# Strided sparse attention and a star-ReLU feed-forward: v of the second batch ahead of three quarters of w_out, the first batch's band q and k by head pair, PSUM banks taken as they come free

## The chip, the core and the metric

The kernel runs on one core of a Trainium2 chip. A core has a matrix engine (TensorE, PE in the profile; PEld are its weight loads), a vector engine (VectorE, DVE), a scalar engine (ScalarE, ACT), GpSimd (POOL) and a sync engine (SyncE, SP). Each engine works through its own list of instructions in order, and they wait for each other by semaphores. POOL and SP issue the DMAs here, each on a queue of its own (q0 for POOL, q1 for SP). Matmuls write to PSUM, which has eight banks of 128 partitions x 512 fp32 numbers. The metric is the device time of one execution in microseconds (us).

## The reference

Inputs are q, k, v of 8 batches x 8 heads x 576 positions x 64, weights w_in (512 x 2048) and w_out (2048 x 512), and two numbers s and b. All are fp32.

```python
scores = scale * np.matmul(q, k.transpose(0, 1, 3, 2))
rel = pos[:, None] - pos[None, :]
mask_local = (rel >= 0) & (rel < 32)
mask_strided = (rel >= 0) & (pos[None, :] % 32 == pos[:, None] % 32)
# heads 0 to 3 take mask_local, heads 4 to 7 mask_strided
scores = np.where(mask, scores, -1e9)
attn = exp(scores - max) / (sum + 1e-9)
x = (attn @ v).transpose(0, 2, 1, 3).reshape(4608, 512)
h = x @ w_in
r = np.maximum(h, 0.0)
out = (s * (r * r) + b) @ w_out
```

## The kernel before

**Attention.** A batch has four pairs of heads, m = 0 to 3 (`pair_steps`): two local ("band") pairs and two strided pairs. A band pair is cut into 6 blocks of 96 positions, a strided pair into 8 groups of 72 positions. For each pair PE transposes q and k (`trans`, lines 405 and 413), an engine copies the results from PSUM (q into a block-diagonal tile qD, k into kT), PE computes scores (line 533; in batch 0 after a matmul at line 530 that adds the mask as large negative numbers), ACT takes the exponential (line 551), PE multiplies by v with a column of ones (AV, line 590), DVE takes the reciprocal of the sums (line 605), DVE or ACT scales (lines 616 and 611), PE transposes x (`xtrans`, line 638) and an engine copies it to xT. In later batches some transposes are made by DMA.

**Feed-forward.** The 4608 tokens make 9 blocks of 512. A block's first layer (`ff1`, line 883) is 64 matmuls (16 column groups of w_in times 4 pieces of x); ACT or DVE takes the ReLU (lines 910 and 912) and the square (lines 918 and 920). The second layer (`ff2`, line 941; from block 3 on a scheme with fewer products at line 851) multiplies by w_out. b times the column sums of w_out (`bcs_steps`, lines 968 and 979) is added when the result is taken out of PSUM (line 952), so block 0's results stay in their banks until all of w_out has come. Block 0 needs the x of batch 0 alone; block 1 needs that of batches 0 and 1.

**Order of the work.** A planner (`Plan`) writes the order of all instructions when the program is built. It keeps a clock for PE and estimates of when each engine is free, how long each job takes and when each load lands (`landing`, `arrive`). At each point it emits the first step that is ready by these estimates: attention while it is behind its due time, else first layer, else second layer. Where nothing is ready in the first part of the program, `keep_running` emits filler matmuls (line 1177). A step that opens a group of matmuls needs a PSUM bank. Banks have five tags: t (1 bank), s (2), a (1), f1 (2), f2 (2). `group_of` gives each group one tag, in fixed turns, and within a tag the banks are taken in turn.

**Loads.** POOL issues the loads that convert fp32 to fp16. In the first part its list is: q and k of batch 0's band heads (`load_qk`, line 275, one load of 288 KB each), q, k, v of its strided heads (line 290), a cast of v of heads 0 and 1 (line 317), a small copy at line 1069 that waits for the strided q, w_in in three loads (line 307), a cast of v of heads 2 and 3, and then `second`: w_out chunk 0, q and k of batch 1, w_out chunks 1 to 3 (line 313), v of batch 1 (lines 295 and 290). SP loads v of batch 0's band heads as fp32 (`stage_v`, line 240) into room that w_out fills later: heads 0 and 1 at the start, heads 2 and 3 after a tiny DMA (line 1051) that waits for the band q to land; then the masks, s and b. In tile names this v is called w_out_sb, because it lies there. `ql`, `kl` are band tiles, `qs`, `ks`, `vs` strided ones.

Of the kernel before, what the change touches and what calls it, by code (L numbers as in the profile page):

```python
# [9 lines left out]
FP16 = mybir.dt.float16  # L10
FP32 = mybir.dt.float32
# [4 lines left out]
class Plan:  # L16
# [9 lines left out]
    def __init__(self):  # L26
        self.t = 0.0
        self.done = {}
        self.pend = []
        self.free = {"A": 0.0, "V": 0.0, "P": 7000.0, "D": 0.0, "X": 0.0, "Y": 0.0}  # L30
        self.count = {}

    def ready_at(self, needs):
        if any(k not in self.done for k in needs):
# [6 lines left out]
    def flush(self):  # L41
        while True:
            best = None
            for p in self.pend:
                r = self.ready_at(p[0])
                if r is not None and r <= self.t and (best is None or r < best[0]):
                    best = (r, p)
            if best is None:
                return
            r, p = best  # L50
            self.pend.remove(p)
            eng = min(p[1], key=lambda e: max(self.free[e], r) + p[1][e])
            end = max(self.free[eng], r) + p[1][eng]
            self.free[eng] = end
            p[2](eng)
            for k in p[3]:
                if isinstance(k, Group):
                    k = ("rel", k.tag, k.n)
                soon = isinstance(k, tuple) and k[0] == "soon"
                self.done[k] = end + (6000.0 if soon else p[4] or self.LAT[eng])  # L60

    def step_ready(self, s):
        r = self.ready_at(s.needs)
        if r is None:
            return None
        if s.group is not None:
            n = self.count.get(s.group.tag, 0)
            if n >= s.group.bufs:
                k = ("rel", s.group.tag, n - s.group.bufs)
                if k not in self.done:  # L70
                    return None
                r = max(r, self.done[k])
        return r

    def emit(self, s):
        if s.group is not None:
            s.group.n = self.count.get(s.group.tag, 0)
            self.count[s.group.tag] = s.group.n + 1
        s.fn()
        self.t += s.ns  # L80
        for k in s.keys:
            self.done[k] = self.t + 200.0
        for p in s.posts:
            self.post(*p)
        if s.after is not None:
            s.after()
# [11 lines left out]
class Group:  # L98


    def __init__(self, tag, bufs):
        self.tag, self.bufs, self.n = tag, bufs, None


class Step:
# [6 lines left out]
def kernel(  # L112
# [130 lines left out]
    stage_v(range(2))  # L243
    nc.sync.dma_start(out=negs, in_=h_neg.ap())
    nc.vector.memset(ones16, 1.0)
    nc.vector.memset(part32, 1.0 / 32)
    nc.vector.memset(vl_stage[0:LPAD], 0.0)
    for i in range(2):
        nc.vector.memset(qD_loc[i], 0.0)
        nc.vector.memset(kT_loc[i][:, 0:LPAD], 0.0)  # L250
        nc.vector.memset(qD_str[i], 0.0)
    for i in range(NV):
        nc.vector.memset(v_loc[i][:, :, :, D:D + 1], 1.0)
# [80 lines left out]
    def cast_v(b, loc, mm, key):  # L334
        nt, np_, dst = (LT, 128, v_loc) if loc else (ST, SQ, v_str)

        def g(eng):
            src = vl_stage if loc else loaded[b, "vs"].rearrange(
                "p (h t d) -> p h t d", h=4, d=D)
            for h in range(2 * mm, 2 * mm + 2):  # L340
                copy_on(eng, out=dst[b % NV][0:np_, h, :, 0:D], in_=src[:, h])
        n = nt * D
        plan.post([key], {"P": 1000.0} if loc else {"A": 2 * (170 + 0.83 * n), "V": 540.0}, g,
                  [("cast", b, mm) if loc else ("in", "vs", b, mm)])
        if loc:
            rows_before(b, mm, ("cast", b, mm))

    def rows_before(b, mm, key):
# [5 lines left out]
        def g(eng):  # L354
# [4 lines left out]
    TB, SB, AB, F1B, F2B = 1, 2, 1, 2, 2  # L359
    HEAD_T = 2  # L360
    PE_MASK = 1
    ps = {tag: [psum.tile([128, PS], FP32, name=f"ps_{tag}{i}") for i in range(n)]
          for tag, n in (("t", TB), ("s", SB), ("a", AB), ("f1", F1B), ("f2", F2B))}

    taken = {"a": 0, "t": 0, "s": 0}

    def group_of(kind, b, m, q=False):

        t, a, f1, f2 = ("t", TB), ("a", AB), ("f1", F1B), ("f2", F2B)
        banks = {"a": [a], "t": [t], "s": [("s", SB)]}[kind]  # L370
        if b == 0:
            banks = {"a": [f2, f2, f1], "t": [t, a], "s": [("s", SB), ("s", SB), f1]}[kind]
        elif b == 1 and kind == "a":
            banks = [f1, f1, a]
        elif b >= KB_DMA and kind == "a":
            banks = [a, t]
        elif b == 1 and q:
            banks = [t, f2]
        taken[kind] += 1
        return Group(*banks[taken[kind] % len(banks)])  # L380

    def bank(group):
        return ps[group.tag][group.n % group.bufs]

    def pair_steps(b, m):

# [196 lines left out]
        def av(e, j, group):  # L583
# [13 lines left out]
            if j % per == per - 1:  # L597
# [2 lines left out]
                j0 = j - per + 1  # L600

                def rc(eng):
                    st["rec", e, j] = recp.tile([128, 6, 1], FP32, tag="rec" + group.tag,
                                                bufs=group.bufs, name="rec")
# [386 lines left out]
    def arrive(keys, at):  # L991
        for k in keys:
            plan.done[k] = at
# [81 lines left out]
    for mm, at in (0, 7100.0), (1, 14400.0):  # L1075
# [21 lines left out]

# [64 lines left out]
    def keep_running(until):  # L1162

        ghz = 1.2 if plan.t < 6000 else 2.4
        n = min(int((until - 100.0 - plan.t) * ghz) - 20, 512) // 128
        for tag, bufs in (("f1", F1B), ("s", SB), ("f2", F2B)):
            k = ("rel", tag, plan.count.get(tag, 0) - bufs)
            if k[2] < 0 or plan.done.get(k, until) <= plan.t:
                break
        else:  # L1170
            return False
        if n < 1:
            return False
        out = ps[tag][plan.count.get(tag, 0) % bufs][:, 0:128 * n]

        def f():
            nc.tensor.matmul(
# [90 lines left out]
```

## Time and profile before

| | |
|---|---|
| median of 5 runs | 309.21 us (308.33 to 309.75) |
| the profiled execution | 308.44 us, span 306.7 us |
| PE busy | 298.0 us (97%), 2686 matmuls |
| DVE, ACT, POOL busy | 217.3, 183.9, 93.0 us |
| granted TensorE clock | 1.00 throughout |
| DMA | 37.31 MB moved; mean 122 GB/s over the span |
| filler matmuls (line 1177) | 32, all before 22 us |

The span is the time from the first to the last instruction in the profile; the time of the execution is 1.74 us longer. A PE that is shown busy may hold filler, and short matmuls overlap, so their lengths (about 200 ns) are longer than the distance from one start to the next (some 32 ns for 65 or 72 columns, 216 ns for 512). In a line of the timeline the bracket tells how long the engine sat idle before the instruction and what ended that.

### The profile page before, as it was taken

The numbers are of one execution on the slowest core, as the hardware profiler recorded it, in microseconds if no ns is written. First come the engines' busy times: TensorE is split into PE (matmuls) and PEld (weight loads), VectorE is DVE, ScalarE is ACT, GpSimd is POOL, SyncE is SP. The second block draws the span as 40 slices with busy tenths as digits, with TensorE's granted clock in tenths as the row PEclk, the third lists the DMA queues.
The fourth block names the chain that finished last, engine by engine and source line by source line (L and its number), as shares of the span: only waits on it lengthen the run. The fifth ranks groups of instructions, "written<-read, shape, count | busy, mean of one in ns | idle before, by whom it ended". The sixth has DMA issues, their size and how long they took to land.

```text
span 306.7 us, 6880 instructions
## 1 busy us (share of the span) xinstructions
PE 298.0 (97%) x2686; PEld 206.4 (67%) x2686; DVE 217.3 (71%) x479; ACT 183.9 (60%) x330; POOL 93.0 (30%) x136
## 2 busy tenths in 40 slices
PE   8898999999999999999999999999999999999995
PEld 3764655666555567777567776778888666766884
DVE  6575767799968678539897987688765366737563
ACT  1875856698857795668387945794525445444300
POOL 8561649910960581069205840000000000000000
PEclk9999999999999999999999999999999999999999
DMA  7999999998999799899996999804010200300223
GB/s 132 171 212 206 214 177 168 205 180 143 84 145 174 101 150 124 182 127 123 132 217 130 134 149 179 190 17 136 2 36 32 72 1 34 105 0 2 81 75 121
DMA packets 100795, 37.31 MB, mean 122 GB/s; under 512 B 80874, under 2 KB 97770, under 8 KB 100762
## 3 DMA queue, kind: packets, MB, share of 16 engines
q0 software_dynamic: 57200, 18.08, 59.3%
q1 hardware_dynamic: 43562, 18.78, 31.3%
q8 instruction: 21, 0.34, 0.5%
q14 instruction: 12, 0.10, 0.1%
HBM read 36.86 MB, written 10.32 MB: 154 GB/s over the span
## 4 chain that ended last, share of the span: by engine, by line
PE 85%; DMA 9%; DVE 2%; POOL 1%; issue 1%; ACT 0%; SPq 0%; POOLq 0%
PE ps_f L883 36%; PE ps_f L851 21%; PE ps_f L941 12%; DMA qs<-in_q_dram 5%; PE ps_s L533 4%; PE ps_a L590 2%; DMA w_out_sb<-in_v_dram 2%; DMA ql<-in_q_dram 2%; PE ps_s L851 2%; PE ps_t L413 2%; PE ps_t L590 1%; PE ps_t L851 1%; PE ps_s L941 1%; PE ps_t L638 1%; DVE gT L920 1%
## 5 line engine op out<-in xcount | busy, mean ns | idle before, releaser
L883 PE MATMUL ps_f<-xT,w_in_sb 128*128 128x512 f16 (+4 forms) x696 | 148.1, 340 | 0.1
L910 ACT ACTIVATE u<-ps_f 128x512 f16<-128x512 f32 x138 | 81.6, 596 | 73.2 <-PE ps_f L883 71.7
L883 PEld LDWEIGHTS <-w_in_sb 128*128 128x128 f16 x704 | 71.5, 113 | 32.1 <-issue 0.2
L851 PEld LDWEIGHTS <-gT 128*128 128x128 f16 x512 | 49.1, 98 | 11.5
L920 DVE TENSOR_TENSOR gT<-u 128x1024 f16<-128x1024 f16 x50 | 34.4, 687 | 23.9 <-ACT u L910 23.4
L941 PE MATMUL ps_f<-w_out_sb,gT 128*128 128x512 f16 x176 | 47.9, 379 | 0.3 <-DVE gT L920 0.3
L851 PE MATMUL ps_f<-w_out_sb,gT 128*128 128x256 f16 x312 | 43.4, 273 | 0.0
L941 PEld LDWEIGHTS <-gT 128*128 128x128 f16 x192 | 17.1, 98 | 12.3 <-DVE gT L920 0.4
L616 DVE TENSOR_TENSOR x_nat<-ps_a,rec 72x256 f16<-72x256 f32 (+1 forms) x52 | 23.8, 458 | 0.6
L551 ACT ACTIVATE p_loc<-ps_s 128x384 f16<-128x384 f32 x46 | 20.9, 493 | 4.8 <-PE ps_s L533 3.8
L918 ACT ACTIVATE gT<-u 128x1024 f16<-128x1024 f16 x22 | 23.3, 1057 | 0.6
L551 ACT ACTIVATE p_str<-ps_s 72x432 f16<-72x432 f32 (+1 forms) x46 | 20.7, 482 | 2.0 <-PE ps_s L533 1.7
L295 POOL DMA_DIRECT2D v_loc<-in_v_dram x28 | 20.7, 754 | 3.3 <-DVE qD_loc L317 1.8
L590 PEld LDWEIGHTS <-p_str 72*128 72x128 f16 x256 | 15.5, 98 | 8.7 <-issue 1.2
L723 DVE TENSOR_TENSOR gT<-gT 128x1024 f16<-128x1024 f16 x28 | 18.5, 682 | 2.6 <-ACT gT L918 1.3
L851 PE MATMUL ps_f<-w_mix,gT 128*128 128x256 f16 x144 | 18.3, 272 | 0.0
L851 PEld LDWEIGHTS <-S 128*128 128x128 f16 x160 | 15.4, 98 | 3.4
L605 DVE RECIPROCAL rec<-ps_a 72x4 f32<-72x4 f32 (+1 forms) x52 | 9.1, 175 | 8.5 <-PE ps_a L590 8.4
L1012 POOL COPY gate<-kT 1x1 f16<-1x1 f16 x6 | 1.7, 281 | 43.5 <-DMA kT<-ks 43.5
L300 POOL DMA_DIRECT2D v_str<-in_v_dram x16 | 13.0, 814 | 5.6 <-DMA ks<-in_k_dram 3.2
L723 DVE TENSOR_TENSOR S<-gT 128x1024 f16<-128x1024 f16 x16 | 10.6, 686 | 5.6 <-PE ps_f L851 4.5
L851 PE MATMUL ps_f<-w_mix,S 128*128 128x256 f16 x96 | 13.7, 272 | 0.0
(156 smaller groups left out, 419.2 us busy)
## 6 DMA issues: line engine op xcount, KB each, us to landing
out_dram<-o SPq DMA_DIRECT2D x34, 256.0 KB, 2.2
w_out_sb<-in_moe_w_out_dram POOLq DMA_DIRECT2D x4, 512.0 KB, 11.4
v_loc<-in_v_dram POOLq DMA_DIRECT2D x28, 72.0 KB, 6.9
ql<-in_q_dram POOLq DMA_DIRECT2D x6, 288.0 KB, 6.4
qs<-in_q_dram POOLq DMA_DIRECT2D x6, 288.0 KB, 6.2
ks<-in_k_dram POOLq DMA_DIRECT2D x6, 288.0 KB, 6.9
kl<-in_k_dram POOLq DMA_DIRECT2D x4, 288.0 KB, 7.8
kl<-in_k_dram POOLq DMA_DIRECT2D x16, 72.0 KB, 3.9
```

Of the source, the lines that this page charges most:

```text
L295: nc.gpsimd.dma_start(out=vl[LPAD:128, h, :, 0:D], in_=v_band(b, h))
L300: nc.gpsimd.dma_start(out=vs[:, h, :, 0:D], in_=v[b, 4 + h].rearrange("(p j) d -> p j d", j=ST))
L551: nc.scalar.activation(out=st["pw", g][0:nk, 0:2 * n * nq], in_=st["s", g][0:nk, 0:2 * n * nq], func=AF.Exp, scale=scale)
L590: nc.tensor.matmul(out=st["a"][:, j % per, :], lhsT=st["pw", g][0:nk, i * nq:i * nq + WIDE], rhs=vt[0:nk, 2 * mm + e, j, :])
L616: nc.vector.tensor_tensor(out=st["x"][:, j0:j0 + per, 64 * e:64 * e + 64], in0=st["pa", e, j][0:nq, 0:per, 0:D], in1=st["rec", e, j][0:nq, ...
L723: nc.vector.tensor_tensor(out=at(out), in0=at(x), in1=at(y), op=op)
L851: nc.tensor.matmul(out=gts[name, T, t][:, 0] if halves else gts[name, T][:, t], lhsT=lhs(k, t), rhs=rhs(k), start=fresh and k == 0 and (ha ...
L883: nc.tensor.matmul(out=gts["h", T, ft][:, lo:hi], lhsT=w_in_sb[min(ft // 4, 2)][:, ct].rearrange("p (c x l) -> p c l x", x=128, l=4)[:, ma ...
L910: nc.scalar.activation(out=u, in_=gts["h", T, ft], func=AF.Relu)
L918: nc.scalar.activation(out=g, in_=u, func=AF.Square)
L920: nc.vector.tensor_tensor(out=g, in0=u, in1=u, op=ALU.mult)
L941: nc.tensor.matmul(out=gts[id_], lhsT=gts[T][:, ft, ts * 128:(ts + 1) * 128], rhs=w_out_sb[:, ft, cols], start=(ft == 0), stop=(ft == NFT ...
```

## The change

1. **Banks.** A group no longer has one tag and a turn: it has a list of banks, and when its first step is emitted it takes the one among the free ones that came free first by the planner's clock. The lists are longer than the tags were for batches 0, 1 and 2 and for block 0's feed-forward.
2. **Band q and k of batch 0 by head pair.** Four loads in the order q of pair 0, k of pair 0, q of pair 1, k of pair 1, each of half the size, with an arrival time of its own in the plan. SP's tiny DMA now waits for the second half of q.
3. **v of batch 1** (band and strided) is loaded after batch 1's q and k and before w_out chunks 1 to 3.
4. **Smaller things.** DVE's memsets stand in another order. The casts of batch 0's strided v may also go to POOL. The plan's step that issues w_in waits for the strided q by the plan's clock too. The planner's assumed times change in places. The tile of reciprocals is one set of 8 buffers.

```diff
     def emit(self, s):
         if s.group is not None:
-            s.group.n = self.count.get(s.group.tag, 0)
-            self.count[s.group.tag] = s.group.n + 1
+            free = [x for x in s.group.names if self.banks[x] is not None]
+            s.group.name = min(free, key=lambda x: self.banks[x])
+            self.banks[s.group.name] = None
...
-    nc.vector.memset(part32, 1.0 / 32)
-    nc.vector.memset(vl_stage[0:LPAD], 0.0)
     for i in range(2):
         nc.vector.memset(qD_loc[i], 0.0)
         nc.vector.memset(kT_loc[i][:, 0:LPAD], 0.0)
+    nc.vector.memset(vl_stage[0:LPAD], 0.0)
+    for i in range(2):
         nc.vector.memset(qD_str[i], 0.0)
...
+    nc.vector.memset(part32, 1.0 / 32)
...
     def load_qk(b):
-        for name, src in (("q", q), ("k", k)):
+        for mm in range(2) if b == 0 else ():
+            hs = slice(2 * mm, 2 * mm + 2)
+            for name, src in (("q", q), ("k", k)):
+                if mm == 0:
+                    loaded[b, name + "l"] = inp.tile([LQ, NL], FP16, tag=name + "l", name=name + "l")
+                nc.gpsimd.dma_start(out=h4(loaded[b, name + "l"])[:, hs],
+                                    in_=view_l(src, b)[:, hs])
+        for name, src in (("q", q), ("k", k)) if b else ():
...
-        plan.post([key], {"P": 1000.0} if loc else {"A": 2 * (170 + 0.83 * n), "V": 540.0}, g,
+        plan.post([key], {"P": 1000.0} if loc else {"A": 2 * (170 + 0.83 * n), "V": 540.0,
+                                                           **({"P": 1500.0} if b == 0 else {})}, g,
...
-        t, a, f1, f2 = ("t", TB), ("a", AB), ("f1", F1B), ("f2", F2B)
-        banks = {"a": [a], "t": [t], "s": [("s", SB)]}[kind]
+        t, a, f1, f2, sc = ("t", TB), ("a", AB), ("f1", F1B), ("f2", F2B), ("s", SB)
+        banks = {"a": a, "t": t, "s": sc}[kind]
         if b == 0:
-            banks = {"a": [f2, f2, f1], "t": [t, a], "s": [("s", SB), ("s", SB), f1]}[kind]
+            banks = {"a": f2 + f1 + a, "t": t + a + f2, "s": sc + f1}[kind]
         elif b == 1 and kind == "a":
-            banks = [f1, f1, a]
+            banks = f1 + a
         elif b >= KB_DMA and kind == "a":
-            banks = [a, t]
+            banks = a + t
         elif b == 1 and q:
-            banks = [t, f2]
-        taken[kind] += 1
-        return Group(*banks[taken[kind] % len(banks)])
+            banks = t + f2
+        elif b == 2 and q:
+            banks = t + f1
+        elif kind == "t" and b == 1:
+            banks = t + f1 + a
+        return Group(*banks)
...
     load_qk(0)
     early_v(0)
     plan.free["P"] = 7100.0
-    for name, at in (("q", 6950.0), ("k", 8750.0)):
-        arrive(both(name + "l", 0), at)
-    arrive(both("qs", 0), 10100.0)
-    arrive(both("ks", 0), 11600.0)
-    plan.done["raw", "v", False, 0] = 13800.0
-    after_landing(0, loaded[0, "ql"][0:1, 0:1])
+    plan.free["V"] = 6500.0
+    AT = {"ql0": 5700.0, "kl0": 6800.0, "ql1": 7900.0, "kl1": 8900.0, "qs": 10100.0,
+          "ks": 11600.0, "vs": 13600.0, "vl0": 7100.0, "vl1": 14700.0}
+    for key, at in AT.items():
+        if key[:2] == "vl":
+            continue
+        arrive([("in", key[:2], 0, mm) for mm in range(2) if key[2:] in ("", str(mm))], at)
+    plan.done["raw", "v", False, 0] = AT["vs"]
+    after_landing(0, loaded[0, "ql"][0:1, NL // 2:NL // 2 + 1])
...
-    plan.post([("in", "vl", 0, 0)], {"P": 3300.0}, weights_in, [("w",)])
+    plan.post([("in", "vl", 0, 0)] + both("qs", 0), {"P": 2500.0}, weights_in, [("w",)])
...
         weights_out(range(1))
         fetch_qk(1)
-        weights_out(range(1, 4))
         load_vl(1)
         plan.done["raw", "vl", 1] = landing(3200)
         for mm in range(2):
             rows_before(1, mm, ("raw", "vl", 1))
         early_v(1)
+        weights_out(range(1, 4))
...
-            gr = [Group(*x) for x in (("s", SB), ("s", SB), ("f1", F1B), ("f1", F1B))]
+            gr = [Group("s", SB, "f1", F1B) for _ in range(4)]
...
-            gr = Group("f2", F2B) if T == 0 and ft % 4 < 2 else Group("f1", F1B)
+            gr = Group("f1", F1B, "f2", F2B) if T == 0 else Group("f1", F1B)
```

More of the change, by code (lines that the diff above doesn't have):

```diff
@@ L30, in __init__ @@
         self.free = {"A": 0.0, "V": 0.0, "P": 7000.0, "D": 0.0, "X": 0.0, "Y": 0.0}
-        self.count = {}
+        self.banks = {}
     def ready_at(self, needs):
@@ L57, in flush @@
                 if isinstance(k, Group):
-                    k = ("rel", k.tag, k.n)
+                    self.banks[k.name] = end + self.LAT[eng]
+                    k = ("rel", k)
                 soon = isinstance(k, tuple) and k[0] == "soon"
@@ L66, in step_ready @@
         if s.group is not None:
[L67 to L72, printed above, removed]
+            free = [self.banks[x] for x in s.group.names if self.banks[x] is not None]
+            if not free:
+                return None
+            r = max(r, min(free))
         return r
@@ L98, with __init__ @@
 class Group:
-    def __init__(self, tag, bufs):
-        self.tag, self.bufs, self.n = tag, bufs, None
+    def __init__(self, *tags):
+        self.names = [f"{tag}{i}" for tag, bufs in zip(tags[::2], tags[1::2]) for i in range(bufs)]
+        self.name = None
 class Step:
@@ L361 @@
     PE_MASK = 1
-    ps = {tag: [psum.tile([128, PS], FP32, name=f"ps_{tag}{i}") for i in range(n)]
-          for tag, n in (("t", TB), ("s", SB), ("a", AB), ("f1", F1B), ("f2", F2B))}
-    taken = {"a": 0, "t": 0, "s": 0}
+    ps = {f"{tag}{i}": psum.tile([128, PS], FP32, name=f"ps_{tag}{i}")
+          for tag, n in (("t", TB), ("s", SB), ("a", AB), ("f1", F1B), ("f2", F2B)) for i in range(n)}
+    plan.banks.update({name: 0.0 for name in ps})
     def group_of(kind, b, m, q=False):
-        t, a, f1, f2 = ("t", TB), ("a", AB), ("f1", F1B), ("f2", F2B)
-        banks = {"a": [a], "t": [t], "s": [("s", SB)]}[kind]
+        t, a, f1, f2, sc = ("t", TB), ("a", AB), ("f1", F1B), ("f2", F2B), ("s", SB)
+        banks = {"a": a, "t": t, "s": sc}[kind]
         if b == 0:
-            banks = {"a": [f2, f2, f1], "t": [t, a], "s": [("s", SB), ("s", SB), f1]}[kind]
+            banks = {"a": f2 + f1 + a, "t": t + a + f2, "s": sc + f1}[kind]
         elif b == 1 and kind == "a":
-            banks = [f1, f1, a]
+            banks = f1 + a
         elif b >= KB_DMA and kind == "a":
-            banks = [a, t]
+            banks = a + t
         elif b == 1 and q:
-            banks = [t, f2]
-        taken[kind] += 1
-        return Group(*banks[taken[kind] % len(banks)])
+            banks = t + f2
[4 more added lines that the diff above has]
+        return Group(*banks)
     def bank(group):
-        return ps[group.tag][group.n % group.bufs]
+        return ps[group.name]
     def pair_steps(b, m):
@@ L602, in rc @@
                 def rc(eng):
-                    st["rec", e, j] = recp.tile([128, 6, 1], FP32, tag="rec" + group.tag,
-                                                bufs=group.bufs, name="rec")
+                    st["rec", e, j] = recp.tile([128, 6, 1], FP32, tag="rec", bufs=8,
+                                                name="rec")
                     nc.vector.reciprocal(out=st["rec", e, j][0:nq, 0:per],
@@ L1073, in weights_in @@
             arrive([("w_in", c) for c in keys], landing(cost))
-    for mm, at in (0, 7100.0), (1, 14400.0):
+    for mm, at in (0, AT["vl0"]), (1, AT["vl1"]):
         plan.done["raw", "v", True, 0, mm] = at
         cast_v(0, True, mm, ("raw", "v", True, 0, mm))
-    plan.post([("in", "vl", 0, 0)], {"P": 3300.0}, weights_in, [("w",)])
+    plan.post([("in", "vl", 0, 0)] + both("qs", 0), {"P": 2500.0}, weights_in, [("w",)])
     def weights_out(chunks):
@@ L1165, in keep_running @@
         n = min(int((until - 100.0 - plan.t) * ghz) - 20, 512) // 128
[L1166 to L1170, printed above, removed]
+        free = [x for x in plan.banks if x[0] in "fs" and plan.banks[x] is not None
+                and plan.banks[x] <= plan.t]
+        if not free:
             return False
@@ L1173, in keep_running @@
             return False
-        out = ps[tag][plan.count.get(tag, 0) % bufs][:, 0:128 * n]
+        out = ps[free[0]][:, 0:128 * n]
         def f():
```

## The prediction

> **What bounds the kernel now.** The page's first part gives PE 298.0 us busy of 306.7, so time can be won only where PE does nothing useful. I cut the span into stretches (busy time by stretch; per engine: busy us, instructions; then granted clock, DMA share, GB/s):
>
> ```profile
> 0.00:6.50 6.50, 5.44 (x13) 1.94 (x14) 4.72 (x19) 1.28 (x1) 5.43 (x13) 1.00 0.70 118
> 13.00:15.00 2.00, 1.57 (x32) 1.41 (x30) 1.96 (x7) 1.86 (x5) 1.05 (x2) 1.00 0.46 76
> 15.00:26.00 11.00, 10.36 (x139) 7.26 (x138) 7.54 (x26) 7.80 (x21) 4.94 (x8) 1.00 1.18 211
> 26.00:34.00 8.00, 6.60 (x73) 3.49 (x71) 4.95 (x8) 6.05 (x10) 2.58 (x5) 1.00 1.22 205
> 34.00:42.00 8.00, 8.00 (x83) 5.56 (x84) 6.56 (x12) 6.35 (x15) 3.88 (x6) 1.00 1.24 201
> 82.00:88.00 6.00, 5.03 (x42) 2.71 (x40) 4.95 (x14) 5.25 (x10) 6.00 (x9) 1.00 0.79 102
> 88.00:300.00 212.00, 211.87 (x1802) 153.20 (x1801) 149.50 (x310) 120.99 (x206) 41.67 (x61) 1.00 0.81 101
> ```
>
> The reader sees two regimes: from 34 us on PE is full but for 1.0 us at 82 to 88; before it is not, and the DMA runs at about 205 GB/s from 15 to 42 us, with a hole at 13 to 15. So the change can act on the first 34 us, and only by moving PE work into them. Next the timeline of PE there (start, length, instruction, count):
>
> ```profile
> 1.06 6.78 PE L1177 MATMUL ps_f<-w_mix 128*128 128x512 f16 x18 [1.06 <-DVE w_mix L245]
> 7.76 0.45 PE L405 MATMUL ps_a<-ident,ql 96*64 96x96 f16 x12
> 10.12 0.45 PE L405 MATMUL ps_t<-ident,kl 96*64 96x96 f16 x12
> 14.34 0.25 PE L533 MATMUL ps_s<-qD_str,kTs 128*72 128x144 f16 x1 [0.42 <-DVE kTs L317]
> ...
> 24.58 4.91 PE L883 MATMUL ps_f<-xT,w_in_sb 128*128 128x512 f16 x22
> 30.37 0.45 PE L405 MATMUL ps_f<-ident,ql 96*64 96x96 f16 x12 [0.88 <-DMA ql<-in_q_dram]
> 34.00 0.42 PE L413 MATMUL ps_f<-ident,qs 72*128 72x72 f16 x8 [0.52 <-DMA qs<-in_q_dram]
> ```
>
> L1177 is filler that keeps PE running; real work starts at 7.76. By 34 us, 43 of the 64 first-layer matmuls (L883) of block 0 are done; the other 21, at 216 ns from start to start, fill the stretch after 34. Last the queue of POOL, which issues the loads:
>
> ```profile
> 10.34 2.29 POOL L307 DMA_DIRECT2D w_in_sb<-in_moe_w_in_dram  x3
> 26.71 0.56 POOL L313 DMA_DIRECT2D w_out_sb<-in_moe_w_out_dram  x1 [4.63 <-DMA w_in_sb<-in_moe_w_in_dram]
> 29.17 0.55 POOL L313 DMA_DIRECT2D w_out_sb<-in_moe_w_out_dram  x1 [1.89 <-DMA w_out_sb<-in_moe_w_out_dram]
> 30.61 0.53 POOL L313 DMA_DIRECT2D w_out_sb<-in_moe_w_out_dram  x1 [0.89 <-DMA ql<-in_q_dram]
> 32.94 3.17 POOL L295 DMA_DIRECT2D v_loc<-in_v_dram  x4 [1.80 <-DVE qD_loc L317]
> ```
>
> Each issue waits for the landing of the one eight places ahead. Landings (issue plus time to landing in the trace): w_in 19.06, 21.25, 26.43; batch 1's ql 30.32, kl 32.35, qs 33.86, ks 35.27; w_out chunks 1 to 3 37.19, 40.00, 42.65; v of batch 1 45.36 (band) and 47.18 (strided).
>
> **The change part by part.** *Batch 0's q, k by head pair.* POOL issues four loads instead of two: at 0.60 to 0.70 each (the 32 KB part of qs took 0.60, the whole kl 0.71) 2.6 us for 1.55, so qs, ks, vs, and the first cast of v on POOL (6.26 to 8.26) move 1.05 later. Bytes and their order up to qs are as before, and qs landed 6.65 us after its issue, so backlog hides this; were the queue issue-bound instead, 1.05 us at 104 to 150 GB/s (2 to 5 us) against 200 costs about 0.5. I take 0.2, inside the delay term below. The first halves of q and k should land near 5.3 and 6.5 (half of the bytes before 6.57; 6.57 itself), the last at 8.56 as kl did. The code plans the first transposes at 5.70; they were planned at 6.95 before and ran at 7.76, 0.81 later, behind filler. So real work starts near 6.5.
> A rule of the Trainium skill speaks against the split (DMA: Bandwidth & Descriptors, "Anatomy of one DMA"): each GpSimd-issued load has a fixed part of about 2.0 us, and large loads should be preferred. Taken serially, two more would cost 4 us and turn the gain below into a loss of 1.6, an estimate from that page. In the trace ql, kl, qs landed 1.99 and 1.49 apart at 288 KB each, and the two parts of ks 0.37 apart: fixed parts overlap here, and the sum goes by the rows.
> *Banks as they come free.* kl landed at 8.56, but pair 0's part of it waited for bank ps_t, held by q of pair 1 (DVE copy 8.51 to 10.03), until 10.12. With a free bank: q copy on ACT 6.9 to 8.2 (1.28), k copy 0.64, first band scores at 8.9 instead of 10.76. Pair 1 gains nothing (k at 8.56, q copy behind pair 0's exponentials: scores near 11.3). Strided pairs: ks landed 11.61, transposes 0.26, copy 0.46, so scores near 13 instead of 14.34 and, with both pairs' banks open, about 14 instead of 17.07. ACT's work from there (6 exponentials at 0.40 to 0.55 in place of waits, v cast 1.13, copies) ends near 17 instead of 20.33; the tail after the last exponential took 2.7 us (20.33 to the end of the xT copy, 23.04). So batch 0's x is whole near 19.7. Lending f1 to batch 2's transposes costs nothing while second-layer work stands ready; uncovered, each loan stalls PE by up to 0.65, the longest wait for a chain in the later trace (at 83.4).
> *The gate on SP* now waits for the second half of ql: near 7.6, not 6.57, so v of heads 2 and 3 lands up to 1.0 after 13.81, POOL's cast (1.83) ends near 16.8 instead of 15.77, and pair 1's AV, which ran at 18.18, still finds it. The POOL issues behind it (w_out chunk 0, batch 1's q, k) move by as much, covered by w_in's bytes until 26.43. Not shown by the trace is whether the hole at 13 to 15 us, and w_in behind it, moves too: w_in was issued at 10.34 yet fell in after that hole. Between 0 and 1.0; I take 0.3, since its own wait (qs landed 10.05) hardly moves.
> *Memsets, free times, shared reciprocal tile, the offer of v_str's cast to POOL.* The qD memset ends earlier, part32 (0.17) goes last and is first read at 51 us: nothing. A cast taken by POOL (about 1.2 by its v_loc casts) delays the next one by that: within the 1.4 us to 18.18.
> *First-layer work.* PE can run L883 from 19.7. By 26.43 that is 31 matmuls (6.73 / 0.216) against 24; after that the last w_in chunk has landed and 8.0 us to 34.4 hold 1.1 us of batch 1's transposes and 32 more. So 63 by 34.4 against 45 before (43, and 2 that the transposes of 34.0 to 34.4 are worth): 18 x 0.216 = 3.9 us gained.
> *v of batch 1 ahead of three w_out chunks.* The queue is full there, so landings trade places: v from 35.27 takes 2.7 and 1.8 as before, near 38.0 and 39.8; w_out chunks near 42.3, 44.9, 47.5; q of batch 2 again near 48. From 34.4 to 42.3 (7.9 us) PE has batch 1's attention (5.9: 1.05 transposes, 2.0 scores, 1.8 AV, 1.05 x transposes, by their start-to-start) and chunk 0's second layer (8 x 0.216 = 1.7), 7.6 in all: 0.3 us idle if all is in time, 2.1 if the strided AV and half the x transposes slip past 42.3. I take 1.2, midway, as v lands at 39.8 and its casts and reciprocals still follow. Without the reordering v would land at 45 and idle would be some 3 us more.
> *The stall at 82 to 88* (1.0 us) hangs on the order that the planner writes; it may go, or one like it come: between +1.0 and -1.0, taken as 0.
> **Sum:** 3.9 - 1.2 - 0.3 = 2.4 us. The profiled execution took 308.44 (span 306.7 and 1.74 around it), so it would take 306.0; it lies 0.77 under the median of 309.21, from which 306.8. All bounds together give a gain of 3.9 - 2.1 - 1.0 - 1.0 = -0.2 to 3.9 - 0.3 + 1.0 = 4.6.
>
> **Rivals.** *Nothing to measure.* w_in slides by the full 1.0 and batch 1's attention slips: 3.9 - 2.1 - 1.0 = 0.8, so 308.4, to about 309.5 with a new stall. For it: everything from 15 to 42 us hangs on one full queue. Against: w_in's issue waits on qs alone.
> *Slower: the late w_out chunks.* The row sums need chunk 3, and until they are done (matmul L979 at 51.34, 8.7 us after chunk 3 landed at 42.65) they and block 0's outputs hold the f2 and s banks, so batch 2's scores can't run. With chunk 3 at 47.5 that is 56.2. From 42.3 to there, 13.9 us, PE has 40 second-layer matmuls (8.6), sums (1.9: L968, L979) and rests of attention (1.8), 12.3; the rest must be block 1's first layer, which needs all of batch 1's x. Before, its last x transposes ran at 60.70, 13.5 us after v landed at 47.18; the same lag after 39.8 gives 53.3, in time. It decides from 54.6 on, and turns the sign when x comes 3.3 us later still: 310.5 to 312. For it: the lag was long and the margin is 1.3 us. Against: the wider choice of banks for AV and x transposes shortens the lag.
> *More than forecast.* The stall at 82 goes and batch 1's attention is in time: 304.6, down to 303.6 if the hole at 13 closes too.
>
> **How the numbers follow.** Forecast (305.2 to 308.2) 0.58, more than that 0.10, nothing 0.15, slower 0.17. 0.3% is 0.93 us, about what a measurement of this kernel can tell from no change: faster is under 308.28: 0.58 + 0.10 = 0.68; same 0.15; slower 0.17. Likeliest 306.8; the range 304.2 to 310.3 leaves out half of the case above it and about half of the slower one.
>
> **What would show it.** Right: first L405 before 7 us; strided scores by 13.5; L883 without a break from about 20; over 55 of block 0's 64 by 34.4; v landing near 38 and 40, w_out chunk 3 near 47.5; PE idle under 2 us between 34 and 48. Wrong: w_in landing a microsecond later; a wait of PE for v or w_out at 38 to 48; new waits of PE after 50 for DVE or banks; or strided exponentials still ending past 19, with L883 still starting at 22.

## The result

| | median | executions | lowest to highest |
|---|---|---|---|
| before | 308.76 us | 56 | 307.91 to 311.24 |
| after | 306.62 us | 32 | 305.16 to 310.95 |

The ratio is 0.9935 [0.9921, 0.9948]: 2.0 us faster. The profiled execution of after took 307.4 us (span 305.5), 0.8 above its median, and that of before 308.44, 0.3 below its own; so the two traces, laid beside each other, account for 1.2 us of span and not for the whole gain.

The stretches of after, cut as those of before were (busy us of PE, PEld, DVE, ACT and POOL, each with its instructions; then granted clock, DMA share, GB/s):

```profile
0.00:6.50 6.50, 5.45 (x16) 1.82 (x18) 4.72 (x19) 1.28 (x1) 5.40 (x13) 1.00 0.73 125
13.00:15.00 2.00, 1.96 (x41) 1.80 (x37) 1.81 (x5) 2.00 (x6) 1.41 (x3) 1.00 1.26 160
15.00:26.00 11.00, 10.28 (x109) 6.62 (x110) 7.60 (x24) 7.80 (x23) 5.77 (x10) 1.00 1.13 199
26.00:34.00 8.00, 6.37 (x59) 3.25 (x57) 3.83 (x6) 4.87 (x9) 2.76 (x4) 0.96 1.42 193
34.00:42.00 8.00, 8.00 (x81) 5.38 (x81) 6.26 (x12) 6.61 (x14) 7.08 (x11) 0.82 1.31 161
82.00:88.00 6.00, 6.00 (x56) 3.45 (x55) 4.12 (x11) 4.87 (x8) 5.70 (x8) 1.00 0.97 135
88.00:300.00 212.00, 211.91 (x1801) 153.31 (x1798) 147.46 (x303) 125.90 (x211) 44.33 (x65) 1.00 0.80 102
```

Three things differ from before. PE was idle for 0.97 us at 82 to 88 and no longer is. At 26 to 34 it is not fuller but emptier (6.37 busy for 6.60). And at 34 to 42 it is shown full, but at a granted clock of 0.82. The timeline of PE in after (start, length, instruction, count, idle before) tells of the early steps and of the stall:

```profile
1.05 5.45 PE L1191 MATMUL ps_s<-w_mix 128*128 128x512 f16 x13 [1.05 <-DVE w_mix L246]
6.43 0.45 PE L418 MATMUL ps_t<-ident,ql 96*64 96x96 f16 x12
8.91 0.26 PE L546 MATMUL ps_s<-qD_loc,kT_loc 128*128 128x192 f16 x1 [0.33 <-ACT kT_loc L327]
13.66 0.25 PE L546 MATMUL ps_f<-qD_str,kTs 128*72 128x144 f16 x1
...
23.46 6.64 PE L896 MATMUL ps_f<-xT,w_in_sb 128*128 128x512 f16 x30
31.39 0.45 PE L418 MATMUL ps_t<-ident,ql 96*64 96x96 f16 x12 [1.29 <-DMA ql<-in_q_dram]
33.20 0.56 PE L418 MATMUL ps_f<-ident,kl 96*64 96x96 f16 x12 [0.34 <-ACT qD_loc L327]
34.24 0.69 PE L418 MATMUL ps_t<-ident,kl 96*64 96x96 f16 x12
34.86 1.04 PE L896 MATMUL ps_f<-xT,w_in_sb 128*128 128x512 f16 x2
```

(In after, L1191 is the filler, L418 and L426 the transposes of q and k, L546 scores, L896 the first layer, L564 the exponential, L624 and L629 the scaling, L651 the transposes of x, L954 and L864 the second layer.) The head of the kernel is earlier, as was meant. But after a first-layer matmul that started at 29.72 us PE, working down its written order, came to the transposes of batch 1's q, which landed only at 31.34, and stood there although 20 of the 64 first-layer matmuls of block 0 were still to do: 44 had started by 30 us. Then from 33.39 to 36.80 the records show a clock of 0.5. In this execution these two took back what the earlier head had won.

A ledger for the whole span: the distance from each matmul's start to the next start, less its nominal time (0.42 ns a column, from 82 ns for 192 columns and 216 for 512 in these traces, and a few ns; 23 to 30 ns for the shortest), with filler counted as lost in full, summed by stretch. It is my own calculation from the traces, in us; what is not lost is 289.8 to 290.6 in every kernel of the table, so the sum explains the span of that one execution. It doesn't always stand for the median: the profiled execution of after lies 0.8 us above its median, those of "no free banks", "1.2 earlier" and "2.4 later" 1.0, 1.5 and 2.1 below theirs.

| profiled execution | 0–26 | 26–34 | 34–42 | 42–64 | 64–100 | over 100 | sum | span |
|---|---|---|---|---|---|---|---|---|
| before | 11.75 | 2.37 | 0.01 | 0.30 | 1.47 | 0.42 | 16.3 | 306.7 |
| after | 10.67 | 2.89 | 1.33 | 0.29 | 0.09 | 0.41 | 15.7 | 305.5 |
| batch 1 planned 1.2 later | 9.87 | 1.04 | 1.59 | 0.46 | 0.55 | 0.15 | 13.7 | 303.5 |
| v not first | 10.24 | 2.23 | 0.11 | 1.46 | 1.45 | 0.02 | 15.5 | 305.6 |
| no split | 12.12 | 2.54 | 0.01 | 2.97 | 0.63 | 0.47 | 18.7 | 309.1 |
| no free banks | 11.80 | 1.84 | 0.64 | 0.23 | 0.10 | 1.26 | 15.9 | 306.2 |
| batch 1 planned 1.2 earlier | 10.90 | 3.33 | 0.74 | 0.35 | 0.08 | 2.61 | 18.0 | 308.3 |
| batch 1 planned 2.4 later | 12.53 | 0.00 | 1.39 | 2.17 | 0.08 | 0.02 | 16.2 | 306.8 |
| 1.2 later and v not first | 9.58 | 1.03 | 0.10 | 3.73 | 2.47 | 6.21 | 23.1 | 313.1 |

From before to after: 1.1 won in the head, 0.5 lost at 26 to 34, 1.3 lost at 34 to 42, 1.4 won at 64 to 100. Of the 1.2 us of span this places 0.6; the rest lies in the nominal times.

### The profile page after: what moved, and what is told of

It reads as the page before. It is cut to its first block, busy times and chain, and to the rows that moved or that the text cites. A ratio compares the mean times of both kernels' runs of the same rounds, so it can differ in the third digit from the quotient of the medians.

```text
span 305.5 us, 6791 instructions
## 1 busy us (share of the span) xinstructions
PE 298.5 (98%) x2676; PEld 206.7 (68%) x2676; DVE 213.8 (70%) x471; ACT 190.0 (62%) x337; POOL 97.2 (32%) x142
## 4 chain that ended last, share of the span: by engine, by line
PE 88%; DMA 7%; POOL 3%; DVE 1%; issue 1%; ACT 0%; POOLq 0%
PE ps_f L896 38%; PE ps_f L864 20%; PE ps_f L954 13%; PE ps_s L546 5%; DMA ql<-in_q_dram 5%; PE ps_a L603 3%; DMA vs<-in_v_dram 2%; PE ps_s L864 2%; PE ps_t L603 1%; PE ps_t L864 1%; PE ps_s L954 1%; PE ps_t L426 1%; PE ps_t L651 1%; PE ps_f L426 1%; POOL v_loc L327 1%; PE ps_a L864 1%
## 5 line engine op out<-in xcount | busy, mean ns | idle before, releaser
L896 PE MATMUL ps_f<-xT,w_in_sb 128*128 128x512 f16 (+4 forms) x696 | 148.8, 341 | 0.0
L896 PEld LDWEIGHTS <-w_in_sb 128*128 128x128 f16 x704 | 71.5, 113 | 33.5 <-issue 0.5
L864 PEld LDWEIGHTS <-gT 128*128 128x128 f16 x512 | 49.4, 98 | 11.7
L954 PE MATMUL ps_f<-w_out_sb,gT 128*128 128x512 f16 x176 | 49.0, 379 | 0.0
L933 DVE TENSOR_TENSOR gT<-u 128x1024 f16<-128x1024 f16 x44 | 30.6, 696 | 24.2 <-ACT u L923 23.5
L864 PE MATMUL ps_f<-w_out_sb,gT 128*128 128x256 f16 x312 | 42.9, 273 | 0.0
L931 ACT ACTIVATE gT<-u 128x1024 f16<-128x1024 f16 x28 | 29.6, 1059 | 0.8
L629 DVE TENSOR_TENSOR x_nat<-ps_a,rec 72x256 f16<-72x256 f32 (+1 forms) x55 | 25.3, 460 | 0.9
L954 PEld LDWEIGHTS <-gT 128*128 128x128 f16 x192 | 17.2, 98 | 11.7 <-issue 1.2
L564 ACT ACTIVATE p_loc<-ps_s 128x384 f16<-128x384 f32 x46 | 20.6, 491 | 4.9 <-PE ps_s L546 4.5
L564 ACT ACTIVATE p_str<-ps_s 72x432 f16<-72x432 f32 (+1 forms) x45 | 20.3, 482 | 4.1 <-PE ps_s L546 3.8
L603 PEld LDWEIGHTS <-p_str 72*128 72x128 f16 x256 | 15.5, 98 | 8.2 <-issue 0.6
L618 DVE RECIPROCAL rec<-ps_a 72x4 f32<-72x4 f32 (+1 forms) x55 | 9.8, 179 | 14.4 <-PE ps_a L603 14.2
L864 PE MATMUL ps_f<-w_mix,gT 128*128 128x256 f16 x144 | 18.6, 273 | 0.0
L864 PEld LDWEIGHTS <-S 128*128 128x128 f16 x160 | 15.5, 98 | 3.7
L327 ACT COPY qD_loc<-ps_t 64x576 f16<-64x576 f16 x18 | 11.4, 632 | 6.7 <-PE ps_t L418 5.1
```

The costliest lines, as they stand in the source:

```text
L564: nc.scalar.activation(out=st["pw", g][0:nk, 0:2 * n * nq], in_=st["s", g][0:nk, 0:2 * n * nq], func=AF.Exp, scale=scale)
L603: nc.tensor.matmul(out=st["a"][:, j % per, :], lhsT=st["pw", g][0:nk, i * nq:i * nq + WIDE], rhs=vt[0:nk, 2 * mm + e, j, :])
L629: nc.vector.tensor_tensor(out=st["x"][:, j0:j0 + per, 64 * e:64 * e + 64], in0=st["pa", e, j][0:nq, 0:per, 0:D], in1=st["rec", e, j][0:nq, ...
L864: nc.tensor.matmul(out=gts[name, T, t][:, 0] if halves else gts[name, T][:, t], lhsT=lhs(k, t), rhs=rhs(k), start=fresh and k == 0 and (ha ...
L896: nc.tensor.matmul(out=gts["h", T, ft][:, lo:hi], lhsT=w_in_sb[min(ft // 4, 2)][:, ct].rearrange("p (c x l) -> p c l x", x=128, l=4)[:, ma ...
L931: nc.scalar.activation(out=g, in_=u, func=AF.Square)
```

## The experiments

Two theories. **A, the wait:** the head's gain is real, and what holds it down is that PE gets to batch 1's q before the DMA does; move that step in the written order and the gain grows. **B, the order:** each part of the change, and each small shift of an assumed time, makes the planner write another order for the whole program, so that parts can't be priced one by one and any of them may bring or remove stalls far away. (The recorded expectations below each explain what they call A and B; these are not always the two named here.)

**Batch 1's loads planned 1.2 us later.** The loads themselves don't move; the planner only believes that they land later.

```diff
     def second():
+        nonlocal ring
+        ring += 1200.0
         fetch_qk(1)
```

> The changed kernel, but the planner takes batch 1's q, k, v and the last three w_out chunks to land 1.2 us later (the loads themselves are issued as before). Theory A (PE's 1.67 us wait for batch 1's ql at 29.7 to 31.4 us, and the half clock that follows it, eat the head's gain): PE does first-layer work there instead, the granted clock stays at 1.00 through 34 to 42 us, and the time is 1 to 2.5 us under the changed kernel's 306.6, 304.1 to 305.6, with less scatter. Theory B (the full DMA queue decides; the wait only moves to kl, qs or v): 306.2 to 307.0.

Measured: 305.74 us (305.38 to 306.28, 4 executions), ratio to before 0.9903 [0.9884, 0.9921]. The stretches 26 to 34 and 34 to 42 of its profile:

```profile
26.00:34.00 8.00, 8.00 (x86) 4.53 (x85) 4.16 (x7) 6.61 (x12) 3.89 (x6) 1.00 1.38 194
34.00:42.00 8.00, 7.14 (x89) 4.90 (x87) 7.86 (x18) 7.42 (x16) 6.64 (x10) 1.00 1.22 162
```

PE is full at 26 to 34, the wait for ql is gone, the clock is 1.00 throughout, and 56 first-layer matmuls have started by 34 us, for 48. PE then runs out of work for 0.86 us at 34 to 42, which is the idle stretch that the prediction had there. What A said of the wait, the first-layer work and the clock is seen in this trace; the time, 305.74, lies between the two ranges. That the gain comes from the wait is not shown: the order behind is another one too, and w_in's last part landed at 26.05 here and at 27.16 in the profiled execution of after, with the same order of loads, so part of the 2.0 us between the two spans is that. By the medians it is 0.9 us better than after; its slowest time, 306.28, is beaten by 11 of after's 32, so what it takes away is mostly after's slow tail, as far as four executions can tell.

**The same step planned 1.2 us earlier**, to double the wait (q and k of batch 1 only; the times behind are as before).

```diff
     def second():
+        nonlocal ring
+        ring -= 1200.0
         fetch_qk(1)
+        ring += 1200.0
```

> The changed kernel, but the planner takes batch 1's q and k to land 1.2 us earlier than it did (the loads are issued as before), so PE's wait for ql gets longer by about 1 us. If that wait and the half clock after it cost what the trace suggests: lost time at 26 to 42 us up by 1 to 2 us, a clock under 1.00 there, 307.5 to 309, wide scatter. If PE only gives back idle time that it would have had later anyway: within 0.5 us of 306.6.

Measured: 311.64 us (309.41 to 315.89), ratio 1.0085 [1.0056, 1.0114]. From the timeline of its PE:

```profile
31.19 0.45 PE L418 MATMUL ps_t<-ident,ql 96*64 96x96 f16 x12 [2.18 <-DMA ql<-in_q_dram]
183.96 1.03 PE L864 MATMUL ps_f<-w_out_sb,gT 128*128 128x256 f16 x8 [1.81 <-DVE Va L783]
```

The wait grew by 0.9 us and the median by 5.0, past the 309 expected at most. The second line is a stall of 1.8 us for DVE at 184 us (Va is a tile that DVE makes for the second layer), which after doesn't have: of the added loss in the ledger 0.4 lies at 26 to 34 and 2.2 behind 100 us. The mean clock was 0.987 to 0.995 in 9 of its 12 executions (one stretch of 3.41 us at half clock in 305 makes 0.994, two make 0.989); it was so in 6 of 32 of after, and in 3 of the 84 of before that ran beside the experiments. So the kernel with the longer wait is slower, as A says, but most of the price isn't the wait, and the profiled execution, 1.5 us under the median, shows only a part of it.

**Planned 2.4 us later.**

```diff
     def second():
+        nonlocal ring
+        ring += 2400.0
         fetch_qk(1)
```

> The changed kernel with batch 1's q, k, v and the last w_out chunks planned 2.4 us later (twice the shift of the 1.2 us run, which gave 305.74). If the shift only has to cover the loads' real lateness (ql was planned for 30.0 and landed at 30.0 to 31.3), the second 1.2 us bring nothing: 305.3 to 306.3, no half clock, no wait for ql. If PE work now starts late for want of a plan, batch 1's attention slips and PE idles at 38 to 48: 306.3 to 308.

Measured: 310.77 us (308.43 to 312.4), ratio 1.0058 [1.0028, 1.0088], slower than either expectation. Nothing is lost at 26 to 34, but 2.2 us at 42 to 64, and the head has a stretch at half clock (19.80 to 23.22 us, up to 1.7 of the 1.9 us that the head loses more than after's):

```profile
15.00:26.00 11.00, 9.46 (x101) 6.25 (x101) 5.73 (x22) 6.46 (x22) 5.87 (x10) 0.84 1.07 185
```

The mean clock was under 0.996 in 8 of 9 executions. From 1.2 earlier over no shift and 1.2 later to 2.4 later (the first moves q and k alone) the medians are 311.6, 306.6, 305.7, 310.8: 1.2 us to either side of the two good ones costs 5.0 us. So sharp a dependence fits B.

**The same shift of 1.2 us in the kernel before.**

> The kernel before with the same 1.2 us later plan for batch 1's loads and nothing else. Its PE waited 0.88 us for ql and 0.52 for qs. If those waits are worth what they last and the change has a worth of its own: 307.3 to 308.2. If the later plan is most of what the changed kernel needs and its own parts add little: 305.7 to 306.7. If first-layer work is what the wait would have delayed anyway: 308.5 to 309.2.

Measured: 308.87 us (308.03 to 311.62), ratio 1.0029 [1.0006, 1.0052]. Before waited 0.88 us for ql too, and this shift brought it nothing, as the third expectation had it: in its trace 1.3 us less is lost at 26 to 34 (1.09 for 2.37), and 0.7 and 2.0 more at 34 to 42 and 42 to 64. What was won in one stretch was given back in the next two. That v comes after w_out there, so that the work to fill the gap runs out sooner, would fit; it wasn't tested apart.

**Filler in the wait.** Seven filler matmuls (128x512, 1.5 us, nobody reads them) ahead of the first transpose of batch 1's q, to see whether the half clock is the price of the wait.

```diff
+                if (b, m, name, j) == (1, 0, "q", 0):
+                    for _ in range(7):
+                        nc.tensor.matmul(out=bank(group), lhsT=ones16,
+                            rhs=ones16[:, None, :].to_broadcast([128, 4, 128]),
+                            start=True, stop=True)
```

> The changed kernel with seven filler matmuls (1.5 us of work that nothing uses) just ahead of the first transpose of batch 1's q, where PE waits for the load. If the half clock after the wait is what makes some executions slow: no execution with a mean clock of 0.995 or less, the upper tail over 307 gone, median 305.5 to 306.5 in spite of the added work. If the wait alone counts and the clock does not: same scatter as the changed kernel, 306.6 to 307.5, the filler adding up to 1.5 us where ql comes in time.

Measured: 307.31 us (306.36 to 314.61), ratio 0.9969 [0.9944, 0.9993]: no better than after. In its profiled execution the clock at 26 to 42 is 1.00, but half of its 12 executions have a mean clock of 0.988 to 0.994. So keeping PE busy in this one wait doesn't keep the clock up over the whole execution, and which other stretch drops is not seen, since only one execution of each kernel is profiled.

**One part undone.** v after w_out again; whole q and k loads again (with the old assumed times and SP's old wait); fixed banks in turns again.

```diff
         fetch_qk(1)
+        weights_out(range(1, 4))
         load_vl(1)
...
-        weights_out(range(1, 4))
```

> The changed kernel, but v of batch 1 is loaded after all of w_out, as before. By the prediction v lands near 45 us and PE idles some 3 us more between 34 and 46: 308.5 to 310. Rival (first-layer work left over after 34 us and chunk 0 to 3 of the second layer cover the late v, as in the kernel before): within 0.7 us of 306.6.

Measured: 308.07 us (306.18 to 309.25), ratio 0.998 [0.9961, 0.9998]: less than the one expectation and more than the rival allowed.

```diff
-        for mm in range(2) if b == 0 else ():
+        for mm in ():
...
-    AT = {"ql0": 5700.0, "kl0": 6800.0, "ql1": 7900.0, "kl1": 8900.0, "qs": 10100.0,
+    AT = {"ql": 6950.0, "kl": 8750.0, "qs": 10100.0,
...
-    after_landing(0, loaded[0, "ql"][0:1, NL // 2:NL // 2 + 1])
+    after_landing(0, loaded[0, "ql"][0:1, 0:1])
```

> The changed kernel, but batch 0's band q and k come as two whole loads, planned as before (6.95 and 8.75 us), and SP's gate waits for the whole q as before. By the prediction the first band scores go back by about 1.5 us, of which w_in's landing hides a part: 306.8 to 308. Rival (the strided pairs set the end of batch 0, and they do not depend on it): 306.2 to 306.9. If the slide of w_in by 0.7 us comes from the later SP gate, w_in's last part lands near 26.4 again.

Measured: 311.24 us (309.37 to 313.25), ratio 1.008 [1.005, 1.0111]: slower than before, and 3 us past the upper end of what was expected.

```diff
-            banks = {"a": f2 + f1 + a, "t": t + a + f2, "s": sc + f1}[kind]
+            banks = {"a": [f2, f2, f1], "t": [t, a], "s": [sc, sc, f1]}[kind]
...
-        return Group(*banks)
+        taken[kind] += 1
+        return Group(*banks[taken[kind] % len(banks)])
```

> The changed kernel, but each group of matmuls gets one PSUM tag in fixed turns, as before. By the prediction batch 0's x is whole 2 us or more later (near 22 instead of 20.9 us) and most of the head's gain goes: 307.6 to 309. Rival (the gain is the stall at 82 to 88 us that the new order happens to lack): the time goes with that stall alone, 306.6 without it in the trace, about 308 with it.

Measured: 308.94 us (306.77 to 310.89), ratio 1.0011 [0.9989, 1.0033], as expected; its trace lacks the stall at 82 to 88 us too, so the rival, 306.6 without that stall, falls. Without free banks the last strided exponential ends at 19.96, for 17.53 in after and 20.33 before. Undoing v costs 1.5 us, the banks 2.3, the split 4.6; they add up to 8.4 where the whole change is worth 2.1. The ledger shows where time is lost, though not the whole of the medians: without v first 1.2 us more goes at 42 to 64, where batch 1's x is whole at 62.9 and not 56.1, and 1.4 more at 64 to 100, for 1.9 less at 26 to 42, which in this pair of executions makes no difference in sum; without the split 1.5 more in the head, but 2.7 more at 42 to 64, where no load is late (v from 36.2 to 39.4, w_out to 47.7). For the banks it doesn't tell: the profiled execution loses 0.2 more than after's, 1.1 more in the head and 0.9 more behind 100 us for 1.7 less at 26 to 42.

**One part alone**, in the kernel otherwise as before: the split with the smaller things, the banks, v first. Each is after with the other parts undone by the edits above.

> Of the change only the split of batch 0's band q, k (and the smaller things: memsets, planner's times); banks in fixed turns and v behind all of w_out, as before. Theory A (the split and the free banks each bring PE work into the first 26 us, so the lost time of PE there falls): lost time before 26 us about 0.5 us under the kernel before, 308.0 to 308.6. Theory B (what each part is worth is the order that the planner happens to write afterwards): anywhere between 307 and 311, with the difference in PE's waits after 42 us, not before 26.

> Of the change only the banks taken as they come free (and the smaller things); band q, k in whole loads, v behind all of w_out. Theory A: strided scores and exponentials end earlier (last strided exponential near 19.5 us instead of 20.33), 307.8 to 308.6. Theory B: the lost time before 26 us stays near the 11.75 of the kernel before, and the total goes with waits after 42 us, 307 to 311.

> Of the change only v of batch 1 ahead of three w_out chunks (and the smaller things). In the head nothing is faster, so 20 or more first-layer matmuls are still there after 34 us and cover a late v anyway: theory A says 0 to 1.5 us slower than before (w_out late, banks held longer), 308.8 to 310.3. Rival (an earlier v ends batch 1's attention earlier and spares the stalls between 48 and 88 us): 307.3 to 308.3.

Measured: split 309.26 us, 1.0015 [0.9999, 1.003]; banks 310.89 us, 1.0065 [1.0037, 1.0093]; v first 308.79 us, 0.9999 [0.9982, 1.0016]. None gains alone, one loses 2. The split and the banks miss what A expected and lie in B's wide range; v first lies between its two. In the head the reason can be seen: with the split alone the last strided exponential ends at 20.28, with the banks alone at 20.39, and only with both at 17.5. For the whole time B fits: no part shows a price of its own. One stretch has a rule all the same. In the eight traces with v of batch 1 first, its x is whole at 53.1 to 56.1 us and PE is not idle at all at 64 to 100 us in six of them and 0.31 and 0.69 us in the other two; in the six with v behind w_out, x is whole at 61.7 to 63.3 and PE is idle there for 0.43 to 1.84. So the stalls between 64 and 100 us go with v first, as the rival recorded for "v first" alone had it; how the one leads to the other was not traced, and v first alone gives most of it back elsewhere.

**The better plan without v first**: 1.2 us later, and v after w_out.

> The changed kernel with the plan 1.2 us later and v of batch 1 again behind all of w_out: what v first is worth once PE no longer waits for ql. If v first shields against idle PE at 38 to 48 us as the prediction had it: 307 to 309 (305.74 with v first). If first- and second-layer work covers a late v: 305.4 to 306.4.

Measured: 314.61 us (312.04 to 316.14), ratio 1.0192 [1.0149, 1.0234], far past both expectations. Up to 42 us its ledger is the best of the table (10.7 lost); 12.4 us goes behind, with a line like this in the timeline of PE:

```profile
197.60 0.60 PE L864 MATMUL ps_f<-w_out_sb,gT 128*128 128x256 f16 x4 [2.69 <-DVE Va L783]
```

PE isn't idle at 34 to 42 though v lands at 43 to 47 there: w_out's chunks, landed at 36.6 to 42.5, give it second-layer work. The loss came at 50 us and after, in waits for DVE and ACT, among them this 2.7 us at 197 us in a part of the program that the edits don't name, and in two stretches of 3.41 us at half clock, from 61.86 and from 198.39 us, which cost up to 1.6 us each in the ledger. That the order written there differs is certain; why the planner's order is so much worse there was not traced, nor why "no split" loses 2.7 at 42 to 64. Both stay open.

## Why the prediction was right, and where only its sum was

The forecast of 306.8 us stands beside 306.62 measured. The steps did not all hold.

**The split and the free banks, up to the exponentials: right.** First real work predicted at 6.5, measured 6.43; SP's wait 7.6 and 7.62; band scores 8.9 and 8.91; strided scores 13 and 13.66, about 14 and 14.98 for the second pair; last strided exponential 17 and 17.53, for 20.33 before. The halves landed at 5.57, 6.88, 7.62 and 8.87, 0.7 to 1.3 us apart, so the two added loads cost no serial fixed time: the serial reading that was weighed there would have had 4 us.

**The tail after the last exponential: wrong, 4.0 us for 2.7**, so batch 0's x was whole at 21.5 and not 19.7. ACT in after, from the last exponential on:

```profile
17.14 0.40 ACT L564 ACTIVATE p_str<-ps_s 72x288 f16<-72x288 f32 x1
17.50 1.72 ACT L624 ACTIVATE x_nat<-ps_f,rec 72x64 f16<-72x64 f32 x8
19.09 0.66 ACT L327 COPY xT<-ps_t 128x576 f16<-128x576 f16 x1
19.60 0.96 ACT L624 ACTIVATE x_nat<-ps_f,rec 72x64 f16<-72x64 f32 x4
20.86 0.64 ACT L327 COPY xT<-ps_f 128x576 f16<-128x576 f16 x1 [0.30 <-PE ps_f L651]
```

Before, the first strided pair was scaled while the second still waited for banks, and only four of ACT's scalings (0.91) came after the last exponential. Now the last exponentials of the two pairs end 1.9 us apart (15.65 and 17.53; before 16.13 and 20.33), and 12 of the scalings (2.68) stand in the tail. The stall that the split and the banks removed had been covering that work.

**The term of 3.9 us, 63 matmuls by 34.4: wrong in size.** By 26.43 there were 28 (31 predicted), by 34 there were 48: a gain of 5 over the 43 of before, or 1.1 us. The step "8.0 us hold 1.1 us of transposes and 32 more" left out that the order is written: PE stopped at ql with first-layer work in hand. Its own sign, over 55 by 34.4, did not come. Planned 1.2 later, PE made 56 by 34 and 57 by 34.4, a gain of 13 or 2.8 us by 34; of the 6 that still lack at 34.4, batch 0's x explains 4 to 5 (whole at 20.69 there, 1.0 later than forecast).

**The delay of w_in, 0.3 between 0 and 1.0: inside.** In the profiled execution of after the last part came 0.73 later (27.16 for 26.43) and ql 1.02 later; in others with the same order of loads w_in came at 26.05, 26.40 and 27.31, so it varies by more than the term, and the hole at 13 to 15 us is sometimes filled (160 GB/s in after, 64 and 86 in two of the experiments). It is the lateness of ql against the planner's 30.0 that mattered, which the prediction had in no term.

**v against w_out: right in the landings, not in the idle time.** v landed at 37.7 and 39.7 (38.0 and 39.8 predicted), w_out at 43.4, 45.9 and 48.3 (42.3, 44.9, 47.5). PE isn't idle at 34 to 42 (1.2 predicted); 1.3 goes to the half clock there instead. The sentence that without the reordering some 3 us more would be idle there fell: both kernels with v behind w_out lose 0.1 at 34 to 42, and pay after 42.

**The slower rival** did not come in. Batch 1's last x transposes ran at 53.5 (53.3 predicted), inside the 54.6 from which it was to decide; ACT's copy made x whole only at 56.1, past it, and still 0.3 us is lost at 42 to 64. The row sums and block 0's outputs ran at 53.9 and not 56.2, and there was second-layer work until block 1's first layer began at 59.1.

**The stall at 82 to 88, taken as 0: it went**, which gives 1.4 in the ledger at 64 to 100. By the traces most of it goes with v first, for which the prediction had no such term. So the sum came out by luck: a term that was left at zero came in at its good end, while the main term came in short. In the profiled execution the ledger adds up to 0.6 us and not 2.4. The medians differ by 2.1, from 308.76 and not from the 309.21 that the forecast started from; 26 of after's 32 executions kept a clock of 0.998 or more, and their median is 306.5 (the other six: 308.5). Where those 26 win their time was not traced, since the one that was profiled is among the six.

## What to carry to other kernels

Where the order is fixed when the program is built, a saving early in the program is only worth what the written order can do with it: ask which wait the engine now reaches too soon, and check the planner's assumed landing against the trace before anything else. Try parts together and not only one by one, since a rewritten order moves stalls to places that the edit doesn't name; a change of 1.2 us in one assumed time moved the changed kernel by 1 to 5 us, and the kernel before by 0.4 the wrong way. And a tail measured behind a stall is too short a price for the same tail without the stall.

## What the runs showed of the hardware that was not expected

PE's clock halved without PE having been idle for long. In the 13 traces whose records hold the clock, every slow stretch begins a whole number of 3.41 us after the record's first entry, and that entry stands at another place in each trace (3.8 to 6.8 us). Cut by this grid, the window ahead of after's slow stretch, and that stretch, are:

```profile
29.98:33.39 3.41, 1.78 (x36) 1.02 (x37) 1.86 (x3) 1.86 (x3) 1.41 (x2) 1.00 1.40 196
33.39:36.80 3.41, 3.41 (x39) 2.14 (x34) 1.65 (x3) 1.82 (x4) 2.78 (x5) 0.50 1.92 97
```

The first has PE busy for 1.78 of 3.41 us, with no idle time over 1.3 us; then the records show half the clock for 3.41 us. The Trainium skill (TensorE: Matmul & The Clock Gate, "Part 1: The HAM clock gate") says that the clock falls after an idle window of about 3.4 us, and that these windows run free of the program. The length of the slow stretch and the grid agree; the condition doesn't, since a window half busy was enough here. Nor is it the share of busy time alone. Two windows of the "1.2 earlier" kernel, as busy as that one or less, kept the full clock behind them, and one of the "2.4 later" kernel, two thirds busy, was followed by half clock:

```profile
27.25:30.66 3.41, 1.76 (x9) 0.68 (x6) 0.79 (x2) 1.49 (x3) 1.42 (x2) 1.00 1.20 197
180.85:184.27 3.42, 1.61 (x21) 1.39 (x19) 3.42 (x9) 0.00 (x0) 1.76 (x3) 1.00 1.41 192
16.39:19.80 3.41, 2.24 (x48) 1.84 (x45) 3.31 (x16) 3.25 (x15) 3.11 (x6) 1.00 1.11 176
```

One count parts them: the columns of each matmul at 0.42 ns, times the share of the 128x128 array that its weights fill (0.375 for a transpose of 96x64). By it the eight windows that were followed by half clock in these 13 traces, four of them at the end of the program, hold 0 to 0.33 of a window's full work, and all 1134 other whole windows 0.35 or more. It was found in the traces afterwards, as one of several counts, and no run was made to test it. The wait in after then costs its own 1.3 us and, where its window falls under that mark, up to 1.7 more (half of 3.41), and that is one part of why after's executions scatter by 5.8 us. It doesn't explain all of it: four executions of after at 308.5 to 309.4 us had a mean clock of 1.00.
